# Sixteen maxima rounds of a gated mix kernel moved into a stage between the first up pairs

## The chip, the cores and the metric

The kernel runs on one core of one Trainium2 chip. The metric is the device time of one execution in microseconds. A core has five engines with a queue of instructions each: PE (TensorE, products; its weight loads are shown as PEld), DVE (VectorE), ACT (ScalarE), POOL (GpSimd) and SP (SyncE, which here issues nearly all DMAs). An engine works through its queue in program order, and an instruction waits on semaphores that other engines or DMAs raise.

## The reference

Input x has 2048 rows of 576. The output is `g * a + (1 - g) * b`:

```
g = sigmoid((x * gate_w).sum(-1))
a = softmax(q k^T * 18 ** -0.5) v @ wo          # 32 heads of 18; q, k, v = x @ wqkv
b = gelu(layernorm(x) @ w1 + b1) @ w2 + b2      # 576 -> 4608 -> 576, tanh form of gelu
```

All is float32.

## The kernel before, in words

A float32 product is made of three products of fp32r parts: each operand is split into a rounded part and the rest (`hh` and `hl`, or `t[:, 0]` and `t[:, 1]` of a weight), and rest times rest is left out.

**Front part** (to 250 us): four blocks `tb` = 0 to 3 of 512 rows. Each block has nine qk groups (lines 752 to 770: 14 products, the split by ACT and DVE, two writes to `qk_scr`) and eight v groups (lines 772 to 791: 14 products each, one tile of v written to `v_scr` after every second group). Between them the next block's x is transposed (line 687), the rows are normalized, and the normalized rows y are transposed, split and written to `y_scr` (lines 707 to 717, five `y_chunk`s a block).

**Maxima rounds.** The softmax needs each row's maximum ahead of the exponential. A round (`s1_round`, line 187) makes two score products of 512 columns (line 199) into the three banks of `ps_s1`, and DVE reduces each to maxima (line 201). There are 32 units (a pair of heads, half of the rows) of 32 rounds. After a unit's last round its maxima are transposed (line 216), read by ACT (line 218, tile `mr`) and written as rows into `qa` by DMA. The table `ROUNDS` puts the first 40 rounds into the front part: 10 in block 1, 14 in block 2, 16 in block 3, where they stand between the groups and share `ps_s1` with the transpositions. The other 984 stand in the loop.

**Loop** (from 250 us): 512 steps. A step makes two score products of 512 columns twice (`s2`, line 240, into the one two-bank tile `pss`) and their exponentials on ACT (line 242); every second step makes the products with v (`pv`, line 257). Rounds and pieces of the MLP stand between them.

**MLP** (`mlp`, line 326): a generator that yields after each slot of work with an estimate of its time; the loop takes pieces from it and paces them so that it ends at step 506 (`fill`, `behind`, `TOTAL`). For each of 36 chunks there are two *up pairs* (`h_pair`: two tiles of 512 columns of the hidden layer, 27 slots of two products at line 445) and four *out pairs* (`out_pair`, line 525). An up pair needs its split weight `W1[q]` and both parts of y: Y[0] (rounded) and Y[1] (rest), each a tile `big` loaded from `y_scr`. Y[1] gets the buffer that block 3's x holds until its last v group. After an up pair comes GELU on two tiles: bias (DVE and ACT, lines 465 and 466), Square on ACT, add and multiply on POOL (`plus`, recorded at line 156), Tanh on ACT, add and multiply on POOL, then the split into `hh` and `hl` on POOL. `open_pairs` lets one pair at a time be in GELU.

**Weights of the first 18 pairs** are split here: a raw chunk is loaded (`load_w1`, line 332; `load_w2`, line 338), ACT rounds it and POOL subtracts (`split`, lines 354 to 375, ACT at 361, POOL recorded at line 156). There is one raw tile R1 for W1, so the next chunk is loaded after POOL is done with the last. These steps, and all that is put off by `defer`, are recorded when `run_due` is called, which counts `slot`; in block 3 that is once for each round and once for each group from g = 9.

SP's DMAs use eight semaphores in turn, so a DMA's issue waits until the DMA eight places earlier has landed.

Of the kernel before, what the change touches and what calls it, by code (L numbers as in the profile page):

```python
# [8 lines left out]
F32 = mybir.dt.float32  # L9
# [35 lines left out]
PROJ = 7  # L45
EARLY = NSTEP - 40
ORDER = (0, 1, 3, 2)
ROUNDS = [lambda g: 0, lambda g: int(g >= 7), lambda g: int(g < 14), lambda g: int(g >= 4) + int(6 <= g < 9)]
SKIP = 0
N_AT = 5  # L50
W_AT = {0: 1, 1: 2, 3: 3, 5: 4, 7: 5}
# [5 lines left out]
def gated_mix_kernel(ctx: ExitStack, tc: tile.TileContext, x, wqkv, wo, w1, b1, w2, b2, gate_w, out):  # L57
# [39 lines left out]
    def psum(pool):  # L97
        return pool.tile([P, TB], F32, name="ps")
# [205 lines left out]
    def mlp():  # L304
# [112 lines left out]
        def cuts(n, pieces):  # L417

            return {(k * n + pieces - 1) // pieces for k in range(1, pieces)}

        def h_pair(q, last, inner=False):

            i, m, fc = chunk(q)
            tb = seq[i][0]
            while q == 0 and q not in W1:
                cut[0] = 3
                yield 0
            wt = ready(W1, q)
            del W1[q]
            ps = [psum(ps_w) for _ in range(2)]  # L430
            if q == 0:
                slots = [(w_, 0, c) for c in range(9) for w_ in (0, 1)] + [(0, 1, c) for c in range(9)]
            else:
                slots = [(w_, s_, c) for c in range(9) for w_, s_ in ((0, 0), (1, 0), (0, 1))]
            change = tb + 1 < NB and (q + 1) % (npair // NB) == 0
            loaded = 0
            late = spent[0] < behind[0]
            ends = cuts(27, (5, 5, 4)[piece[0]] if last else (3, 5, 4)[piece[0]])
            if (last or spent[0] > behind[0] + AHEAD) and piece[0] == 0 and not late:

                ends = {4, 9, 14, 18, 23}
            for k, (w_, s_, c) in enumerate(slots):
                for h in range(2):
                    r = slice(64 * h, 64 * h + 64)
                    nc.tensor.matmul(ps[h], wt[w_][r, c, :], Y[s_][r, c, :], start=(k == 0), stop=(k == 26))  # L445
                if change and (k + 1 in ends or k == 26):

                    load_y(tb + 1, 0, loaded, (k + 1) // 3)
                    load_y(tb + 1, 1, loaded, (k + 1) // 3)
                    loaded = (k + 1) // 3  # L450
                if k == 26:
                    break
                if k + 1 in ends:
                    cut[0] = 1
                yield 231
                while k == 25 and open_pairs[0]:
                    cut[0] = 3
                    yield 0
            open_pairs[0] = 1
            if inner:  # L460

                extra = wp1.tile([P, 2, 9, P], F32R, name="w4").rearrange("p a b c -> p (a b c)")
            zs = [zp.tile([P, TB], F32, name="z") for _ in range(2)]
            b = [b1t[:, fc + h:fc + h + 1] for h in range(2)]
            nc.vector.tensor_scalar(zs[1], ps[1], b[1], None, op0=ALU.add)
            nc.scalar.activation(zs[0], ps[0], AF.Identity, bias=b[0])
            for h in (1, 0):
                z = zs[h]
                w = zp.tile([P, TB], F32, name="zz", bufs=3)
                if inner:  # L470
                    hh, hl = [extra[:, (2 * h + k) * TB:(2 * h + k + 1) * TB] for k in range(2)]
                else:
                    hh = hp.tile([P, TB], F32R, name="hh")
                    hl = hp.tile([P, TB], F32R, name="hl")


                def plus(c, w, z):

                    pool_op(TB, nc.gpsimd.tensor_scalar, w, w, c, 1.0, op0=ALU.add, op1=ALU.mult)
                    pool_op(TB, nc.gpsimd.tensor_tensor, w, w, z, op=ALU.mult)  # L480

                def parts(w=w, z=z, hh=hh, hl=hl, h=h, j=2 * m + h):
                    plus(1.0, w, z)
                    rounded(hh, w)
                    pool_op(TB, nc.gpsimd.tensor_tensor, hl, w, hh.bitcast(F32), op=ALU.subtract)
                    queue_end(-1000.0, lambda: HT.update({(i, j): (hh, hl)}))
                    if h == 0:
                        open_pairs[0] = 0

                def first(w=w, z=z, parts=parts):  # L490

                    plus(GC0, w, z)
                    queue_end(200.0, lambda: second(w, parts))

                def second(w, parts):
                    nc.scalar.activation(w, w, AF.Tanh, scale=GC1)
                    defer(2, parts)
                defer(2, lambda w=w, z=z: nc.scalar.activation(w, z, AF.Square))  # L498
                defer(4 - h, first)
            cut[0] = 2  # L500
            yield 231
# [83 lines left out]
        for i in range(n + 1):  # L585
            q = 2 * i
            inside = i < n and seq[i][1] == NG - 1
            held = 1 if 0 < i < n and seq[i][1] == 0 else 2
            if i < n:
# [8 lines left out]
            if i < n and not inside:  # L598
                yield from pair(q + 1, held)

    opening = []
# [21 lines left out]
    def filler(upto):  # L623
# [8 lines left out]
                break  # L632
        run_due()


    mstack = ExitStack()
    with ExitStack() as a:
# [175 lines left out]
        for tb in range(NB):  # L813
            work = [(qk_group, (tb, mt)) for mt in (range(9) if tb < 2 else (4, 0, 1, 2, 3, 5, 6, 7, 8))] + [(v_group, (tb, t, n)) for t in range(4) for n in range(2)]
            for g, (fn, args) in enumerate(work):
# [22 lines left out]
                if tb == NB - 1:  # L838
                    if g == 1:
                        load_k(0, 3 * TB, S)  # L840
                    if g == 2:
                        load_q(1)
                        next(stream[0])
                    if g == 9:
                        qkstack.close()
                        wp1 = mstack.enter_context(tc.tile_pool(name="m_w1", bufs=3))
                        wp2 = mstack.enter_context(tc.tile_pool(name="m_w2", bufs=4))
                        next(stream[0])

# [5 lines left out]
                    if g == 7:  # L855
                        ps = psum(ps_s1)
                        nc.tensor.transpose(ps[:, :NFC], b1r, ident[:NFC, :NFC])
                        nc.vector.tensor_copy(b1t, ps[:, :NFC])
                if tb == 1 and g == 4:
                    load_q(0)  # L860
                    load_k(0, 0, TB)
# [1 line left out]
                    load_k(0, TB, 2 * TB)  # L863
                if tb == 2 and g == 3:
                    load_k(0, 2 * TB, 3 * TB)
                for _ in range(ROUNDS[tb](g)):
                    next_round()
                    run_due()
# [206 lines left out]
    for u in range(NU):  # L1075
        for kc in range(NT):
            step = u * NT + kc
            if kc == 1:
                if u + 2 < NU:
                    load_q(u + 2)  # L1080
                if u % 2 == 0 and u // 2 + 1 < NPAIR - 1:
                    load_k(u // 2 + 1)
                    load_v(u // 2 + 1)
                elif u == NU - 5:
                    load_k(NPAIR - 1)
                elif u == NU - 4:
                    load_v(NPAIR - 1)
            at[0] = step

            next_round()  # L1090
            s2(u, kc, 0)
            run_due(462.0)
            if kc % 2:
                fill(step, 1)
            elif step > 0:
                pv(step - 2)
                while ROWS:
                    ROWS.pop(0)()
                run_due(2080.0)
            if kc % 2:  # L1100
# [36 lines left out]
```

## Time and profile before

| | |
|---|---|
| median of 3 runs | 2357.26 us (2355.15 to 2359.28) |
| profiled execution | 2358.74 us |
| its span | 2356.8 us |
| granted clock of PE, mean | 0.996 |
| PE, DVE, ACT, POOL busy | 98%, 70%, 58%, 41% |

In the views, a row of a timeline has start, duration, engine, line, operation, output tile <- inputs, shapes and count; in brackets stands the engine's idle time before it and what ended that. A row of the table by stages has, for each engine, busy us and the number of instructions, then the granted clock of PE as a share of full speed, the busy share of the DMA engines and GB/s.

### The profile page before, as it was taken

What the parts mean: (1) busy time and instruction counts of PE and PEld (TensorE: products, weight loads), DVE (VectorE), ACT (ScalarE), POOL (GpSimd) and SP (SyncE); (2) the same over time, 40 slices, a digit from 0 to 9 for tenths busy, and PEclk for the clock granted to TensorE, in tenths of its full rate; (3) what the DMA queues carried; (4) which work ended last, traced back from release to release, by engine and by line L of the source; (5) the groups of instructions that cost most, each with busy time, mean ns of one, the idle gap of its engine ahead of it and who ended that gap; (6) DMA issues with size and microseconds to landing.
All of it is one profiled execution on the core that took longest, in us unless ns stands there. A gap on an engine that the chain in (4) does not pass through costs nothing.

```text
span 2356.8 us, 50607 instructions
## 1 busy us (share of the span) xinstructions
PE 2305.6 (98%) x20585; PEld 1613.7 (68%) x20585; DVE 1651.2 (70%) x2890; ACT 1366.8 (58%) x1604; POOL 971.2 (41%) x966
## 2 busy tenths in 40 slices
PE   8998899999999999999999999999999999999999
PEld 6876566666666666676666666666666666666658
DVE  5675577777777777777777777777777777777525
ACT  4222467666666666666665666666666666666661
POOL 4000466666554533333352444444445333333430
PEclk9999999999999999999999999999999999999999
DMA  7746945535455434232444433233354243322345
GB/s 232 248 149 193 275 138 177 175 132 149 135 155 156 157 95 117 95 114 95 127 137 130 160 114 117 94 117 115 117 160 150 94 117 110 102 95 99 131 139 198
DMA packets 164718, 330.40 MB, mean 140 GB/s; under 512 B 57822, under 2 KB 84482, under 8 KB 153650
## 3 DMA queue, kind: packets, MB, share of 16 engines
q1 hardware_dynamic: 161494, 321.71, 43.8%
q10 hardware_dynamic: 2992, 5.46, 0.6%
q8 instruction: 162, 2.65, 0.5%
q14 instruction: 70, 0.57, 0.1%
HBM read 234.31 MB, written 96.73 MB: 140 GB/s over the span
## 4 chain that ended last, share of the span: by engine, by line
PE 88%; DVE 4%; ACT 2%; DMA 2%; issue 2%; POOL 1%; SPq 1%; ACTq 0%; DVEq 0%; POOLq 0%
PE ps L525 20%; PE ps L257 19%; PE ps L445 17%; PE pss L240 13%; PE ps L199 11%; PE ps L763 4%; PE ps L781 2%; DVE m L201 1%; PE ps L1028 1%; ACT p L242 1%; POOL zz L156 1%; PE ps L687 1%; ACT w L361 1%; DMA wraw<-in_B_w_dram 0%; POOL w L156 0%
## 5 line engine op out<-in xcount | busy, mean ns | idle before, releaser
L201 DVE TENSOR_REDUCE m<-ps 128x1 f32<-128x512 f32 x2048 | 1298.3, 684 | 444.3 <-PE ps L199 442.4
L242 ACT ACTIVATE p<-pss 128x1024 f32<-128x1024 f32 x684 | 701.9, 1026 | 459.3 <-PE pss L240 446.8
L156 POOL TENSOR_SCALAR zz<-zz 128x512 f32<-128x512 f32 x288 | 179.7, 624 | 836.3 <-ACT zz L498 737.8
L445 PE MATMUL ps<-big,w 64*128 64x512 f32 x3888 | 520.2, 393 | 3.2 <-DMA big<-y_scr 3.1
L525 PE MATMUL ps<-w,hh 64*128 64x288 f32 x4352 | 495.4, 299 | 11.6
L240 PE MATMUL pss<-qa,ka 56*128 56x512 f32 x2048 | 479.5, 436 | 11.7 <-ACT p L242 7.8
L242 ACT ACTIVATE ring<-pss 128x1024 f32<-128x1024 f32 x340 | 348.9, 1026 | 231.6 <-PE pss L240 226.2
L199 PE MATMUL ps<-ka,qa 54*128 54x512 f32 x2048 | 457.3, 409 | 6.2 <-DVE m L201 2.6
L525 PEld LDWEIGHTS ps<-w,hh 64*128 64x128 f32 x4352 | 396.7, 185 | 67.5 <-issue 44.5
L445 PEld LDWEIGHTS ps<-big,w 64*128 64x128 f32 x3888 | 394.2, 185 | 67.6 <-DMA big<-y_scr 3.8
L156 POOL TENSOR_TENSOR zz<-zz,z 128x512 f32<-128x512 f32 x288 | 372.2, 1292 | 24.0
L240 PEld LDWEIGHTS pss<-qa,ka 56*128 56x128 f32 x2048 | 196.6, 184 | 265.8 <-ACT p L242 126.5
L525 PE MATMUL ps<-w,hl 64*128 64x288 f32 x2176 | 346.7, 292 | 0.0
L257 PE MATMUL ps<-p,vt 128*32 128x512 f32 x2736 | 346.2, 601 | 0.0
L199 PEld LDWEIGHTS ps<-ka,qa 54*128 54x128 f32 x2048 | 239.5, 185 | 36.1 <-DVE m L201 12.0
L525 PEld LDWEIGHTS ps<-w,hl 64*128 64x128 f32 x2176 | 231.4, 185 | 0.5
L156 POOL TENSOR_TENSOR w<-x,w 128x1152 fp32r<-128x1152 f32 (+1 forms) x36 | 73.1, 2045 | 324.8 <-ACT w L361 293.7
L156 POOL TENSOR_TENSOR hl<-zz,hh 128x512 fp32r<-128x512 f32 x136 | 176.9, 1300 | 11.3
L257 PE MATMUL ps<-ring,vt 128*32 128x512 f32 x1360 | 179.1, 598 | 0.0
L257 PEld LDWEIGHTS ps<-p,vt 128*32 128x32 f32 x2736 | 71.5, 109 | 149.0 <-issue 148.6
L534 DVE SCALAR_TENSOR_TENSOR x<-ps,x 128x288 f32<-128x288 f32 x256 | 105.2, 452 | 42.4 <-PE ps L525 28.7
L763 PE MATMUL ps<-big,wqk 128*128 128x512 f32 x504 | 125.2, 401 | 1.1 <-DVE wqk L681 0.9
(95 smaller groups left out, 1368.2 us busy)
## 6 DMA issues: line engine op xcount, KB each, us to landing
w<-w_scr SPq DMA_DIRECT2D x54, 1152.0 KB
w<-w_scr SPq DMA_DIRECT2D x108, 576.0 KB
w_scr<-w SPq DMA_DIRECT2D x18, 1152.0 KB
w_scr<-w SPq DMA_DIRECT2D x36, 576.0 KB
big<-y_scr SPq DMA_DIRECT2D x42, 384.0 KB
x<-in_B_w_dram SPq DMA_DIRECT2D x54, 288.0 KB
qa<-qk_scr SPq DMA_DIRECT2D x192, 72.0 KB
ka<-qk_scr SPq DMA_DIRECT2D x90, 144.0 KB
```

What stands on the lines that cost most here:

```text
L156: fn(*args, **kw)
L199: nc.tensor.matmul(ps, qa[r0:r0 + 54, t * P:(t + 1) * P], ka[r0:r0 + 54, kb * TB:(kb + 1) * TB], start=True, stop=True)
L201: nc.vector.tensor_reduce(M4[u][:, h, t, kb:kb + 1], ps, axis=AX.X, op=ALU.max)
L240: nc.tensor.matmul(ps[:, h, :], ka[r0:r0 + 56, kc * P:(kc + 1) * P], qa[r0:r0 + 56, qb * TB:(qb + 1) * TB], start=True, stop=True)
L242: nc.scalar.activation(RING[n % 3][:, qb], ps, AF.Exp, scale=SCALE)
L257: nc.tensor.matmul(OB[u][r:r + 32, :], v[:, k, 19 * h:19 * h + 32], RING[c % 3][:, qb, h, :], start=(k == 0), stop=(k == NT - 1))
L361: nc.scalar.activation(t[:, 0], src(), AF.Copy)
L445: nc.tensor.matmul(ps[h], wt[w_][r, c, :], Y[s_][r, c, :], start=(k == 0), stop=(k == 26))
L525: nc.tensor.matmul(ps[nn][:, :ND], h_[r, tok], w_[p_][r, cs[nn]], start=(k == 0), stop=(k == 6 * G - 1))
L534: nc.vector.scalar_tensor_tensor(dst, ps[nn][:, :ND], 0.5, b2b[:, cs[nn]] if g == 0 else dst, op0=ALU.mult, op1=ALU.add)
L763: nc.tensor.matmul(ps, w_[:, c, ms], big[:, s_, :], start=(k == 0), stop=(k == len(prods) - 1))
L781: nc.tensor.matmul(ps[:, :ND], big[:, s_, tok], w_[:, c, cs], start=(k == 0), stop=False)
```

## The change

- Block 3 has no rounds (`ROUNDS`). Its 16 rounds stand in a new stage between the front part and the loop: after each round the stage takes two stretches of about 600 ns (by the generator's estimates) from the MLP.
- The first two up pairs are made by `first_pairs`: the 18 slots with Y[0] of pair 0, then those of pair 1, then the nine slots with Y[1] of each. Pair 0 has the two banks of `ps_w`, pair 1 the two-bank tile `pss`. Pair 2 follows by `h_pair` in the same stage.
- GELU is a function of its own, `gelu`. For pairs recorded ahead of the loop (`early`), the two sums stand on ACT, as copies with a bias, instead of POOL.
- b1's transposition moves from block 3 to block 2, two W2 chunks are due three slots later, and step 0 of the loop takes one more piece.

```
-ROUNDS = [lambda g: 0, lambda g: int(g >= 7), lambda g: int(g < 14), lambda g: int(g >= 4) + int(6 <= g < 9)]
+ROUNDS = [lambda g: 0, lambda g: int(g >= 7), lambda g: int(g < 14), lambda g: 0]
...
                 load_w2(c)
+                LOADED[2, c] += 3
...
+        def banks(wide):
+
+            if wide:
+                ps = ps_s2.tile([P, 2, TB], F32, name="pss")
+                return [ps[:, h, :] for h in range(2)]
+            return [psum(ps_w) for _ in range(2)]
+
+        def first_pairs():
+
+            ps = {}
+            for q, slots in ((0, range(18)), (1, range(18)), (0, range(18, 27)), (1, range(18, 27))):
+                while q in (0, 1) and q not in W1:
+                    cut[0] = 3
+                    yield 0
+                if q not in ps:
+                    ps[q] = banks(q == 1)
+                wt = W1[q]
+                for k in slots:
+                    w_, s_, c = (k % 2, 0, k // 2) if k < 18 else (0, 1, k - 18)
+                    for h in range(2):
+                        r = slice(64 * h, 64 * h + 64)
+                        nc.tensor.matmul(ps[q][h], wt[w_][r, c, :], Y[s_][r, c, :], start=(k == 0), stop=(k == 26))
+                    if k < 26:
+                        yield 231
+                if k < 26:
+                    continue
+                while open_pairs[0]:
+                    cut[0] = 3
+                    yield 0
+                del W1[q]
+                yield from gelu(q, ps[q], False)
+                prep(q + 3)
...
+            early = not looped[0]
...
                 def plus(c, w, z):
 
-                    pool_op(TB, nc.gpsimd.tensor_scalar, w, w, c, 1.0, op0=ALU.add, op1=ALU.mult)
+                    if not early:
+                        pool_op(TB, nc.gpsimd.tensor_scalar, w, w, c, 1.0, op0=ALU.add, op1=ALU.mult)
                     pool_op(TB, nc.gpsimd.tensor_tensor, w, w, z, op=ALU.mult)
...
                     nc.scalar.activation(w, w, AF.Tanh, scale=GC1)
+                    if early:
+                        nc.scalar.activation(w, w, AF.Copy, bias=1.0)
...
+                    nc.scalar.activation(w, z, AF.Square)
+                    if early:
+                        nc.scalar.activation(w, w, AF.Copy, bias=GC0)
...
+    def stretch(ns):
+
+        upto = spent[0] + ns
+        while stream and spent[0] < upto:
+            spent[0] += next(stream[0])
+            end, cut[0] = cut[0], 0
+            if end == 3:
+                break
...
     while len(rounds) > NU * NR - NR - 2 * LEAD:
         next_round()
-        run_due()
+        run_due(233.0)
+        for part in range(2):
+            t = spent[0]
+            stretch(600.0)
+            run_due(max(spent[0] - t, 500.0))
```

How the instructions stand in a row shows in two places. The first is PE where the loop began: before, the last products of block 3 (line 784) are followed by block 3's last two rounds (line 199) and the loop's first scores (line 240), and pair 0 (`w_2108` is its weight) comes in pieces of 18 products between the loop's work.

```order
L784 MATMUL ps<-wv_126,big 128x288
L199 MATMUL ps<-ka_106,qa_104 128x512 x4
L240 MATMUL pss<-qa_103,ka_106 128x512 x4
L199 MATMUL ps<-ka_106,qa_104 128x512 x2
L445 MATMUL ps<-big,w_2108 128x512 x18
L199 MATMUL ps<-ka_106,qa_104 128x512 x2
L240 MATMUL pss<-qa_103,ka_106 128x512 x2
L445 MATMUL ps<-big,w_2108 128x512 x18
```

In the changed program (line 837 is the v group's last product, line 443 the product of `first_pairs`, `w_2189` pair 0's weight, `w_2276` pair 1's) the same place reads:

```order
L837 MATMUL ps<-wv_126,big 128x288
L199 MATMUL ps<-ka_106,qa_103 128x512 x2
L443 MATMUL ps<-big,w_2189 128x512 x12
L199 MATMUL ps<-ka_106,qa_103 128x512 x2
L443 MATMUL ps<-big,w_2189 128x512 x12
L199 MATMUL ps<-ka_106,qa_103 128x512 x2
L443 MATMUL ps<-big,w_2189 128x512 x12
L199 MATMUL ps<-ka_106,qa_103 128x512 x2
L443 MATMUL pss<-big,w_2276 128x512 x12
L199 MATMUL ps<-ka_106,qa_103 128x512 x2
```

Pair 1's first product now stands behind four rounds and 36 products; line 240 comes first after 16 rounds and 160 up products.

The second place is SP at the end of the front part. Before, in this order: pair 1's raw W1 (line 332), a raw W2 chunk (line 338), writes of v and y, W2, the rows of unit 0's maxima, and more writes; pair 2's raw W1, two v writes and the six loads of Y[1] (line 111, `big<-y_scr`) come next.

```order
L332 DMA x<-in_B_w_dram 64x9x128 x2
L338 DMA x<-in_B_w_dram 128x576
L791 DMA v_scr<-vt_109 128x832
L715 DMA y_scr<-hh 128x512
L715 DMA y_scr<-hl 128x512
L338 DMA x<-in_B_w_dram 128x576
L111 DMA qa_103<-mr 1x8x128 x4
L715 DMA y_scr<-hh 128x512
L715 DMA y_scr<-hl 128x512
L791 DMA v_scr<-vt_110 128x832
```

In the changed program (line 844 writes v, line 770 the last y chunk), from the last y chunk on:

```order
L770 DMA y_scr<-hh 64x512
L770 DMA y_scr<-hl 64x512
L338 DMA x<-in_B_w_dram 128x576 x2
L844 DMA v_scr<-vt_109 128x832
L844 DMA v_scr<-vt_110 128x832
L111 DMA big<-y_scr 64x3x512 x6
L332 DMA x<-in_B_w_dram 64x9x128 x2
L338 DMA wraw<-in_B_w_dram 128x576 x2
L185 DMA vt_109<-v_scr 128x16x52
L332 DMA x<-in_B_w_dram 64x9x128 x2
```

Pair 1's raw W1 has moved from ahead of the last y writes to behind the six loads of Y[1]; the second line-332 row is pair 2's, which waits until POOL has split pair 1's.

More of the change, by code (lines that the diff above doesn't have):

```diff
@@ L424, in h_pair @@
             tb = seq[i][0]
-            while q == 0 and q not in W1:
-                cut[0] = 3
-                yield 0
             wt = ready(W1, q)
             del W1[q]
[L430 to L434, printed above, removed]
+            ps = banks(False)
+            slots = [(w_, s_, c) for c in range(9) for w_, s_ in ((0, 0), (1, 0), (0, 1))]
             change = tb + 1 < NB and (q + 1) % (npair // NB) == 0
@@ L458, in h_pair, with gelu @@
                     yield 0
+            yield from gelu(q, ps, inner)
+        def gelu(q, ps, inner):
+            i, m, fc = chunk(q)
+            early = not looped[0]
             open_pairs[0] = 1
@@ L496, in second, with square @@
                     nc.scalar.activation(w, w, AF.Tanh, scale=GC1)
+                    if early:
+                        nc.scalar.activation(w, w, AF.Copy, bias=1.0)
                     defer(2, parts)
-                defer(2, lambda w=w, z=z: nc.scalar.activation(w, z, AF.Square))
+                def square(w=w, z=z):
+                    nc.scalar.activation(w, z, AF.Square)
+                    if early:
+                        nc.scalar.activation(w, w, AF.Copy, bias=GC0)
+                defer(2, square)
                 defer(4 - h, first)
@@ L588, in mlp @@
             held = 1 if 0 < i < n and seq[i][1] == 0 else 2
-            if i < n:
+            if i == 0:
+                yield from first_pairs()
+            elif i < n:
                 yield from pair(q, held, last=i > 0)
@@ L597, in mlp @@
                 prep_w2(i)
-            if i < n and not inside:
+            if 0 < i < n and not inside:
                 yield from pair(q + 1, held)
@@ L854, in gated_mix_kernel @@
                         nc.vector.tensor_scalar(gate1, gate, -1.0, 1.0, op0=ALU.mult, op1=ALU.add)
[L855 to L858, printed above, removed]
                 if tb == 1 and g == 4:
@@ L865, in gated_mix_kernel @@
                     load_k(0, 2 * TB, 3 * TB)
+                if tb == 2 and g == 13:
+                    ps = psum(ps_s1)
+                    nc.tensor.transpose(ps[:, :NFC], b1r, ident[:NFC, :NFC])
+                    nc.vector.tensor_copy(b1t, ps[:, :NFC])
                 for _ in range(ROUNDS[tb](g)):
@@ L1099, in gated_mix_kernel @@
                 run_due(2080.0)
+            else:
+                fill(step, 2)
             if kc % 2:
```

## The prediction, made before the changed kernel was run

> **What bounds the kernel now.** I read the page first: engines and the costliest groups. In each row the number before the comma is the group's busy time in us.
>
> ```profile
> PE 2305.6 (98%) x20585; PEld 1613.7 (68%) x20585; DVE 1651.2 (70%) x2890; ACT 1366.8 (58%) x1604; POOL 971.2 (41%) x966
> L445 PE MATMUL ps<-big,w 64*128 64x512 f32 x3888 | 520.2, 393 | 3.2 <-DMA big<-y_scr 3.1
> L525 PE MATMUL ps<-w,hh 64*128 64x288 f32 x4352 | 495.4, 299 | 11.6
> L240 PE MATMUL pss<-qa,ka 56*128 56x512 f32 x2048 | 479.5, 436 | 11.7 <-ACT p L242 7.8
> L199 PE MATMUL ps<-ka,qa 54*128 54x512 f32 x2048 | 457.3, 409 | 6.2 <-DVE m L201 2.6
> L257 PE MATMUL ps<-p,vt 128*32 128x512 f32 x2736 | 346.2, 601 | 0.0
> ```
>
> PE is busy 98% of the span, and the change leaves every one of its products in place. It can win only what PE now loses: idle time and time at a lower clock. So the second view is the table by stages (after the engines: granted clock, DMA share, GB/s).
>
> ```profile
> 195.00:214.00 19.00, 16.43 (x63) 10.68 (x61) 15.39 (x37) 2.48 (x5) 0.00 (x0) 1.00 1.00 221
> 214.00:223.00 9.00, 7.19 (x27) 4.81 (x28) 6.06 (x12) 1.09 (x2) 0.00 (x0) 0.94 0.99 349
> 223.00:235.00 12.00, 9.70 (x54) 8.82 (x53) 5.20 (x12) 5.47 (x9) 5.36 (x3) 0.78 0.27 86
> 250.00:268.00 18.00, 11.91 (x73) 8.29 (x73) 7.45 (x12) 6.57 (x8) 4.96 (x3) 0.86 1.02 241
> 268.00:296.00 28.00, 27.61 (x204) 16.70 (x204) 14.74 (x23) 17.04 (x21) 20.95 (x23) 0.91 0.95 298
> 1000.00:1400.00 400.00, 397.47 (x3777) 272.73 (x3771) 296.61 (x515) 245.08 (x279) 162.99 (x172) 1.00 0.39 120
> ```
>
> In the loop PE idles 2.5 us in 400. The losses lie in block 3 with its 16 rounds (195 to 235: 6.7 us idle, the clock at 0.78 in its last 12) and at the loop's start (250 to 268: 6 us idle, clock 0.86). Just these two places are rebuilt. Note the DMA column: full from 195 to 223 and from 250 on.
>
> **Block 3 without rounds.** Five qk groups stand without a round; v groups stand with a y transposition in block 0 and without one in block 2.
>
> ```profile
> 180.80 16.48 PE L763 MATMUL ps<-big,wqk 128*128 128x512 f32 x70
> 54.45 1.58 PE ps L781 x12
> 56.73 1.59 PE ps L781 x12
> 177.25 1.59 PE ps L781 x12
> 179.12 1.58 PE ps L781 x12
> 250.14 0.59 PE L240 MATMUL pss<-qa,ka 56*128 56x512 f32 x2
> ```
>
> Nine groups at 16.48/5 = 3.3 are 29.7; one transposition 0.5; four v groups at 2.28 and four at 1.87 are 16.6. From 181.0, with 0.5 for the b1 transposition that now stands ahead, the block ends near **228.3** instead of 250.1. Of these 21.8 us, the rounds' own products (32 by 457.3/2048 = 0.223, with their transposition 7.4 in all) only move.
>
> **Break-even.** From 250.1 to the end of the third pair's products, PE does 162 up products at 520.2/3888 = 0.134, 34 of line 240 at 0.234, 32 of line 199 at 0.223 and 48 of line 257 at 0.127: 42.9 us of work.
>
> ```profile
> 291.11 1.56 PE L445 MATMUL ps<-big,w 64*128 64x512 f32 x12
> 292.51 0.40 PE L199 MATMUL ps<-ka,qa 54*128 54x512 f32 x2
> 294.61 1.32 PE L445 MATMUL ps<-big,w 64*128 64x512 f32 x10
> ```
>
> It takes until 295.9, so 2.9 us are lost by these averages. The changed program, up to its first 12 out products (at 495.4/4352 = 0.114), has the same 162, 40 of line 199, 8 of line 240: 34.2 us with the transposition. If it gets there at time t, it stands t - 34.2 + 7.4 - 250.1 - 2.9 = **t - 279.8** us behind before. The stage and the loop's first steps may take until 279.8 before anything is lost.
>
> **What the stage waits for.** PE meets pair 1 after four rounds and 36 products of pair 0, and pair 1's weights are asked for only after the six Y loads. SP's DMAs land in the order of issue: the two halves of Y's first load, issued at 197.6, came at 208.85 and 214.30, when the waits on them ended.
>
> ```profile
> 197.62 1.28 SPq L111 DMA_DIRECT2D big<-y_scr  x2
> 203.80 0.77 SPq L770 DMA_DIRECT2D qk_scr<-hl  x1
> 208.85 0.32 SPq L769 DMA_DIRECT2D qk_scr<-hh  x1
> 214.30 0.32 SPq L770 DMA_DIRECT2D qk_scr<-hl  x1
> big<-y_scr SPq DMA_DIRECT2D x2, 1152.0 KB
> big<-y_scr SPq DMA_DIRECT2D x42, 384.0 KB
> x<-in_B_w_dram SPq DMA_DIRECT2D x54, 288.0 KB
> qk_scr<-hh SPq DMA_DIRECT2D x36, 256.0 KB
> v_scr<-vt SPq DMA_DIRECT2D x16, 416.0 KB
> ```
>
> At 214 some 2.9 MB of qk writes wait (the window 195 to 214 moved 4.2 MB, of which 3.5 are loads). Block 3 still writes y (2.4 MB) and four v tiles (1.7). Before, these were spread to 249; now they are produced by 229. 7.0 MB at the 349 GB/s of the row 214 to 223 take 20 us: to 234. Two W2 chunks (0.59 MB at 221 GB/s) go to 237, Y's second half (2.36 MB; its twin took 5.05 + 5.45 us) to 247.4, pair 1's W1 (0.59 MB) to **250.1**. Then come ACT's rounding and POOL's subtraction:
>
> ```profile
> 249.47 1.17 ACT L361 ACTIVATE w<-x 128x1152 fp32r<-128x1152 f32 x1 [2.75 <-DMA x<-in_B_w_dram]
> 250.71 2.63 POOL L156 TENSOR_TENSOR w<-x,w 128x1152 fp32r<-128x1152 f32 x1 [7.49 <-ACT w L361]
> ```
>
> Pair 1's rounded part is there at 251.3, its rest at 253.9.
>
> **The stage, step by step.** In a stretch without waits an up product starts every 0.117 us (12 in 1.40, rows 291.11 and 292.51) and a round adds 0.24. Pair 0's own W1 split on ACT stands behind the last v eviction, which needs the v tile's write landed (231): rounded part 232.7, rest 235.3. So PE idles to 235.3, works to 240.0, idles to 253.9. Behind the waiting product stand rounds 5 to 16 (so DVE too), pair 0's second part and the exponentials; nothing on PE can pass it. Pair 1's first slots and rounds 5 to 7 end at 261.1, with 2.5 us for a cold clock, as it cost before after the idle stretch at 262:
>
> ```profile
> 268.00:271.00 3.00, 3.00 (x18) 0.59 (x16) 0.00 (x0) 2.06 (x3) 1.56 (x3) 0.50 0.51 153
> 271.00:274.00 3.00, 3.00 (x20) 1.94 (x18) 1.13 (x2) 1.54 (x2) 2.67 (x3) 0.66 1.00 164
> ```
>
> (Three us at 0.50 and three at 0.66 lose 2.5.) The Trainium skill, "TensorE: Matmul & The Clock Gate", part 1, says that an idle window of about 3.4 us halves the clock and a busy one of 3.4 us frees it: an estimate of 1.7 us lost, which would make the sum 0.8 less; the rows above show more.
>
> The Y slots of both pairs end at 266.1, rounds 10 to 12 at 269.5 (they share three banks with the transposition that ACT reads after four GELU steps). Pair 2's weights are loaded once POOL has freed the raw tile at 253.9; by the same rates they land near 258 and are split by 262, in time. Its 52 products and five rounds end near 277.2. Then the exponentials start, each behind GELU steps and behind the next W1's load on ACT:
>
> ```profile
> L242 ACT ACTIVATE p<-pss 128x1024 f32<-128x1024 f32 x684 | 701.9, 1026 | 459.3 <-PE pss L240 446.8
> L156 POOL TENSOR_TENSOR zz<-zz,z 128x512 f32<-128x512 f32 x288 | 372.2, 1292 | 24.0
> L156 POOL TENSOR_SCALAR zz<-zz 128x512 f32<-128x512 f32 x288 | 179.7, 624 | 836.3 <-ACT zz L498 737.8
> L498 ACT ACTIVATE zz<-z 128x512 f32<-128x512 f32 x144 | 82.5, 626 | 0.0
> ```
>
> Four of them (1.03 each), four GELU steps (0.63) and a bias step among them, with 1.2 us of waiting for W1, put the twelfth out product at **t = 286.4**. The eight sums that move cost POOL 8 x 0.624 less and ACT 8 x 0.63 more, if a copy with a bias is priced as its neighbour Square (bounds: nothing, and the exponential's 1.03); they lie beside PE's waits, and without that cover at most 8 x 0.4 = 3.2 us come on top. The b1 transposition, the fill in step 0 and the raised due time of two W2 chunks I price at nothing: PE has other products queued there, or waits anyway. Unit 2's q and k loads move behind the writes of the split weights, but keep their distance to the rounds that use them, which start later as well.
>
> Later the loop has three pairs fewer to do. That is work taken over, counted above; PE's 2.5 us in 400 leave little to win or lose, and I take 0 (bounds -3 and +3).
>
> Sum: 286.4 - 279.8 = **+6.6 us** on the profiled execution's 2358.74, so 2365.3; that execution lay 1.5 above the median of 2357.26. I predict 2365.
>
> **Rivals.** *The stage does its work* (faster). If the queue is empty when Y's load is issued at 229 and everything flows at 349 GB/s, Y and W1 (2.95 MB) land by 237.5 and pair 1 is split by 241.3: t = 273.8, -6.0 us, 2353. It decides from pair 1 being split before 247.3. For it: two of the four idle places of before vanish. Against it: the full DMA column, and Y's halves at 216 to 234 GB/s.
>
> *Reads faster than Y's first load showed*, behind the same writes: 2.95 MB from 237 at 349 GB/s land 4.7 us earlier, +1.9 us, 2361. The waits before also allow it: there W2's chunk, issued right behind Y, was complete 16.0 us after Y's first issue:
>
> ```profile
> 249.67 3.88 SPq L111 DMA_DIRECT2D big<-y_scr  x6
> 265.67 0.68 ACT w L361
> ```
>
> From an issue at 229 that gives 245 and about +1.5. The Trainium skill, "DMA: Bandwidth & Descriptors", Bandwidth, measured 341 GB/s at 1 MB; by that figure, as an estimate, the sum would be +2.1. The trace does not agree so far for 1.18 MB loads.
>
> *The delay spreads* (slower still): a second cold stretch, then GELU of two pairs queued on POOL (about 9 us each by the rows above) ahead of the out products: some 6 us more, +13, 2372.
>
> **Chances.** Forecast (+4.7 to +10) 0.46; reads faster, within 0.2% (4.7 us, about what can be told from no change) 0.30; the stage works 0.12; the delay spreads 0.12. So faster 0.12, same 0.30, slower 0.58. The range from 2352 to 2371 leaves out the far ends of the last two.
>
> **What would show it.** Right: block 3's last v product near 228; PE idle for 10 us or more ahead of the first product into pss by line 443, released by ACT's split of W1; a clock under 0.8 behind it; the first line-240 product at 275 to 280; DMA share near 1 from 195 to 250. Wrong: that product before 247, or a block 3 that ends past 232 because evictions wait for landed writes.

## The result, and the profile after

The changed kernel takes 2372.97 us (median of 4 runs, 2371.89 to 2373.63) and the kernel before beside it 2358.27 (2355.15 to 2360.88): a ratio of 1.0061 [1.0048, 1.0074], 14.7 us slower. Beside later experiments it was run again: 2373.99 us, 1.0064 [1.0051, 1.0077]. The direction was forecast; the 2365 us were 8 short, and the upper bound of 2371 was 2 short.

The profiled execution has a span of 2370.9 us, 14.1 above that of before. The page's engine row:

```profile
PE 2307.9 (97%) x20585; PEld 1619.7 (68%) x20585; DVE 1653.4 (70%) x2890; ACT 1369.7 (58%) x1612; POOL 964.4 (41%) x958
```

PE is busy 2.3 us longer with the same number of products, more of them at a lower clock; the other 11.8 us are idle time. The table by stages, cut at the places that the prediction names:

```profile
195.00:214.00 19.00, 19.00 (x97) 15.99 (x96) 11.60 (x30) 3.09 (x6) 0.00 (x0) 1.00 0.99 212
214.00:229.00 15.00, 14.08 (x106) 13.36 (x104) 5.16 (x11) 6.44 (x12) 2.83 (x2) 1.00 1.05 397
229.00:240.00 11.00, 5.63 (x32) 4.15 (x34) 2.99 (x6) 1.46 (x2) 2.61 (x1) 0.69 1.01 294
240.00:255.00 15.00, 4.51 (x26) 3.01 (x24) 2.54 (x4) 2.31 (x3) 4.83 (x3) 0.67 0.84 172
255.00:275.00 20.00, 18.38 (x118) 13.47 (x118) 14.59 (x26) 9.88 (x16) 11.40 (x10) 0.82 0.84 292
1000.00:1400.00 400.00, 397.52 (x3756) 271.70 (x3754) 297.62 (x514) 246.95 (x280) 162.66 (x172) 1.00 0.41 124
```

Block 3 without rounds runs at full speed: PE is busy 33.1 of 34 us to 229, at a clock of 1.00. Then PE idles 15.9 us in 26, and the clock falls to 0.67. The loop is what it was. PE's timeline of the stage, with the waits in brackets:

```profile
227.74 0.51 PE L199 MATMUL ps<-ka,qa 54*128 54x512 f32 x2
232.47 0.80 PE L443 MATMUL ps<-big,w 64*128 64x512 f32 x2 [4.22 <-ACT w L362]
235.16 2.50 PE L443 MATMUL ps<-big,w 64*128 64x512 f32 x10 [1.90 <-POOL w L156]
...
250.15 0.79 PE L443 MATMUL pss<-big,w 64*128 64x512 f32 x2 [8.59 <-ACT w L362]
252.84 2.50 PE L443 MATMUL pss<-big,w 64*128 64x512 f32 x10 [1.90 <-POOL w L156]
...
277.89 0.62 PE L240 MATMUL pss<-qa,ka 56*128 56x512 f32 x2
...
286.82 0.44 PE L567 MATMUL ps<-w,hl 64*128 64x288 f32 x2
```

And what held pair 1, on ACT: its raw weights landed at 248.9.

```profile
248.93 1.16 ACT L362 ACTIVATE w<-x 128x1152 fp32r<-128x1152 f32 x1 [16.51 <-DMA x<-in_B_w_dram]
```

This is the stage as it was forecast, row by row (below). But it explains half of the 14.1 us. To see where the rest arises, take the **lag**: the start of a step's first exponential, less its start in the kernel before. At step 480 both kernels have done the same products of every kind (counted in the traces), so the lag there needs no correction. Before, then after:

```profile
2176.08 1.02 ACT L242 ACTIVATE p<-pss 128x1024 f32<-128x1024 f32 x1 [0.72 <-PE pss L240]
```

```profile
2183.72 1.02 ACT L242 ACTIVATE p<-pss 128x1024 f32<-128x1024 f32 x1 [0.72 <-PE pss L240]
```

The lag is **7.6 us** at step 480, the spans differ by **14.1**: 6.5 us are lost in the last 32 steps and behind the loop, 1900 us after the stage. The program's order says what differs there: the MLP's last product stands at step 504, not 506, and 70 of the output projection's 448 products by line 1081 stand inside the loop, not 49. The pacing sets that place: it spreads what is left of the MLP over the loop's steps, counted from the work done when the loop begins, and in the runs below its constant alone moves the end between 504 and 506. Which part of the change tipped it (the pairs made early, or the piece more in step 0) no run separates.

### The profile page after: what moved, and what is told of

Read it like the earlier page. It is cut to its first block, busy times and chain, and to the rows that moved or that the text cites. A ratio compares the mean times of both kernels' runs of the same rounds, so it can differ in the third digit from the quotient of the medians.

```text
span 2370.9 us, 50656 instructions
## 1 busy us (share of the span) xinstructions
PE 2307.9 (97%) x20585; PEld 1619.7 (68%) x20585; DVE 1653.4 (70%) x2890; ACT 1369.7 (58%) x1612; POOL 964.4 (41%) x958
## 4 chain that ended last, share of the span: by engine, by line
PE 89%; DVE 4%; DMA 3%; ACT 2%; issue 1%; POOL 0%; SPq 0%; DVEq 0%; ACTq 0%; POOLq 0%
PE ps L567 20%; PE ps L257 19%; PE ps L473 18%; PE pss L240 13%; PE ps L199 11%; PE ps L816 4%; PE ps L834 2%; PE ps L1081 1%; DVE m L201 1%; ACT p L242 1%; DMA x<-in_B_w_dram 1%; DMA qk_scr<-hl 1%; PE ps L740 1%; DVE p L800 0%; DMA dn_scr<-dn 0%
## 5 line engine op out<-in xcount | busy, mean ns | idle before, releaser
L156 POOL TENSOR_SCALAR zz<-zz 128x512 f32<-128x512 f32 x280 | 173.7, 620 | 845.2 <-ACT zz L537 749.9
L473 PE MATMUL ps<-big,w 64*128 64x512 f32 x3780 | 507.5, 393 | 0.0
L473 PEld LDWEIGHTS ps<-big,w 64*128 64x128 f32 x3780 | 386.1, 186 | 59.1
L567 PEld LDWEIGHTS ps<-w,hl 64*128 64x128 f32 x2176 | 235.3, 185 | 0.3
L156 POOL TENSOR_TENSOR w<-x,w 128x576 fp32r<-128x576 f32 (+1 forms) x36 | 73.1, 2042 | 335.7 <-ACT w L362 329.6
```

Source lines behind the costliest of these rows:

```text
L156: fn(*args, **kw)
L567: nc.tensor.matmul(ps[nn][:, :ND], h_[r, tok], w_[p_][r, cs[nn]], start=(k == 0), stop=(k == 6 * G - 1))
```

## The experiments

All twelve runs in one table, below the changed kernel's first. Lag at the end is the span less 2356.8; the column behind it is what was added after step 480. In each of the twelve the products done by step 480 are the same as before. Each lag is read from one profiled execution: two of the changed kernel give 7.6 and 6.9, and y1_split3 and three_mended, whose order is the same up to step 400, differ by 1.4 us at step 384. The intervals of the ratios are 2 to 3 us wide to each side, so the times alone don't tell y1_behind_w1, half_rounds_back and one_pair from the changed kernel; there the timelines decide.

| run | median us | ratio to before | MLP ends at step | lag at 480 | lag at the end | added behind 480 |
|---|---|---|---|---|---|---|
| changed kernel | 2372.97 | 1.0061 [1.0048, 1.0074] | 504 | 7.6 | 14.1 | 6.5 |
| changed_again | 2373.99 | 1.0064 [1.0051, 1.0077] | 504 | 6.9 | 13.2 | 6.3 |
| after_mlp_506 | 2374.62 | 1.0068 [1.0055, 1.0080] | 506 | 15.9 | 17.4 | 1.5 |
| before_mlp_504 | 2364.62 | 1.0024 [1.0015, 1.0033] | 504 | -0.4 | 4.9 | 5.3 |
| tail_506 | 2366.31 | 1.0032 [1.0021, 1.0042] | 506 | 7.6 | 7.7 | 0.1 |
| y1_behind_w1 | 2370.76 | 1.0052 [1.0039, 1.0066] | 504 | 5.5 | 11.3 | 5.8 |
| y1_split3 | 2367.23 | 1.0032 [1.0021, 1.0043] | 504 | 2.8 | 7.8 | 5.0 |
| half_rounds_back | 2369.52 | 1.0046 [1.0034, 1.0059] | 504 | 5.2 | 10.7 | 5.5 |
| one_pair | 2371.51 | 1.0051 [1.0039, 1.0064] | 504 | 4.3 | 14.1 | 9.8 |
| gelu_sums_pool | 2381.48 | 1.0099 [1.0086, 1.0113] | 504 | 17.1 | 23.2 | 6.1 |
| three_mended | 2359.50 | 1.0002 [0.9993, 1.0010] | 506 | 0.7 | 0.3 | -0.4 |
| half_mended | 2358.16 | 0.9997 [0.9988, 1.0006] | 506 | -1.2 | -1.6 | -0.4 |
| half_mended_one_pair | 2356.17 | 0.9990 [0.9981, 0.9999] | 506 | -3.0 | -3.5 | -0.5 |

The theory: the stage costs some 7 us through pair 1's late weights, and the MLP's end at 504 costs some 6 more. The rival: the stage costs all, and the end only shows it.

### The end of the MLP, both ways

after_mlp_506:

```
-FIN = NSTEP - 6
+FIN = NSTEP - 5
```

> The changed kernel with one constant of the pacing moved (FIN = NSTEP - 5), so that the MLP's last product stands at step 506 of 512 again, as in the kernel before, and not at 504; 21 products of the output projection then move from the loop's last steps to behind it. Theory A (about half of the loss was made at the end of the loop: projection products that stand ahead of the last exponentials delay them, and what follows the last exponential is a chain of transfers that doesn't get shorter): 2366 to 2368 us, 5 to 7 below the changed kernel's 2373, and the last exponential about 4 us earlier. Theory B (the whole loss comes from the new stage and its delay is only carried to the end): 2372 to 2374, no difference.

before_mlp_504, on the kernel before:

```
-FIN = NSTEP - 6
+FIN = NSTEP - 8
```

> The kernel before with the pacing constant moved the other way (FIN = NSTEP - 8): the MLP's last product at step 504, as in the changed kernel, and no new stage. Theory A (the end of the MLP at step 504 costs by itself): 2362 to 2365 us, 4 to 7 above the kernel before. Theory B (the end costs nothing, the stage costs all): 2357 to 2359.

The kernel before at 504 costs 5.5 us (2364.62 against 2359.09 beside it), all of it behind step 480: A holds. The changed kernel at 506 did not get faster: 2374.62 us lies outside A's range and 0.6 above B's. Its table row says why: behind step 480 it adds 1.5 us and not 6.5, but ahead of it it lost 8 more. 7.2 of them arise between steps 320 and 384, at both of which it has done the same products as the changed kernel, and one long wait stands there, at step 368. PE, then SP, in after_mlp_506:

```profile
1748.75 1.17 PE L240 MATMUL pss<-qa,ka 56*128 56x512 f32 x2 [4.26 <-DMA qa<-mr]
```

```profile
1729.93 4.22 SPq L111 DMA_DIRECT2D big<-y_scr  x3
1735.41 6.83 SPq L111 DMA_DIRECT2D qa<-mr  x4
```

The same place on SP in the changed kernel, where PE's score product did not wait:

```profile
1724.98 10.22 SPq L111 DMA_DIRECT2D big<-y_scr  x12
1735.30 2.80 SPq L111 DMA_DIRECT2D qa<-mr  x4
```

At the MLP's third change of block, Y is loaded in pieces as its buffers come free. With the other pacing the pair that frees them stands later, the loads run up to the unit's change at step 368, and the four row loads of the new unit's maxima take 6.83 us to issue and not 2.80. The next score product waits 4.26 us and PE then runs at half its clock:

```profile
1740.60:1747.40 6.80, 3.82 (x46) 3.17 (x43) 4.90 (x9) 2.05 (x2) 2.61 (x3) 1.00 1.01 203
1747.40:1754.20 6.80, 5.45 (x22) 1.84 (x24) 0.64 (x1) 1.02 (x1) 0.00 (x0) 0.50 0.02 6
```

So the run mixed two effects. The next one keeps every instruction ahead of step 400 where the changed kernel has it.

tail_506:

```
-            behind[0] = base + (TOTAL - base) * step / FIN
+            behind[0] = base + (TOTAL - base) * step / (FIN if step < 400 else FIN + 1)
```

> The changed kernel with the pacing constant raised by one only from step 400 on, so that every instruction ahead of step 400 stands where the changed kernel has it, and the MLP ends at step 506 in place of 504. The run with the constant raised from the start mixed two things: its end was 6 us shorter, and it got a new 4.3 us wait at step 368, where the block's loads of Y had moved in front of the next unit's four row loads. Theory A (the end of the MLP at 504 costs about 6 us by itself): 2366 to 2368 us, the steps up to 480 within 0.5 us of the changed kernel, and no wait on qa<-mr over 1 us at step 368. Theory B (what the end gives up comes back elsewhere): 2372 to 2374.

2366.31 us, 6.7 below the changed kernel; the lag is 7.6 at step 480 and 7.7 at the end. A holds, B is out: the end costs some 6.5 us by itself. How it costs them, the last steps show. On ACT, the changed kernel:

```profile
2304.42 1.02 ACT L242 ACTIVATE p<-pss 128x1024 f32<-128x1024 f32 x1 [0.65 <-PE pss L240]
2305.34 1.66 ACT L1014 ACTIVATE big<-x 128x512 fp32r<-128x512 f32 x3
2307.84 0.63 ACT L1014 ACTIVATE big<-x 128x512 fp32r<-128x512 f32 x1 [0.84 <-DVE x L1011]
2308.38 1.01 ACT L242 ACTIVATE p<-pss 128x1024 f32<-128x1024 f32 x1
```

and tail_506:

```profile
2301.72 1.02 ACT L242 ACTIVATE p<-pss 128x1024 f32<-128x1024 f32 x1 [0.66 <-PE pss L240]
2303.40 1.03 ACT L242 ACTIVATE p<-pss 128x1024 f32<-128x1024 f32 x1 [0.66 <-PE pss L240]
```

The projection's preparation (line 1014) begins two steps earlier and stands on ACT ahead of the last exponential, which starts 4.0 us after the one before it and not 1.7. Then SP's queue, the changed kernel and the kernel before:

```profile
2316.69 0.38 SPq L982 DMA_DIRECT2D x<-ot_scr  x1
2317.12 0.68 SPq L982 DMA_DIRECT2D ka<-ot_scr  x1
2317.90 0.66 SPq L281 DMA_DIRECT2D dn_scr<-dn  x1
2326.85 0.64 SPq L286 DMA_DIRECT2D ot_scr<-dn_scr  x1
```

```profile
2304.49 0.35 SPq L281 DMA_DIRECT2D dn_scr<-dn  x1
...
2307.66 0.65 SPq L286 DMA_DIRECT2D ot_scr<-dn_scr  x1
2308.42 0.43 SPq L929 DMA_DIRECT2D x<-ot_scr  x1
2308.90 0.70 SPq L929 DMA_DIRECT2D ka<-ot_scr  x1
```

The last unit's softmax sums (`dn`, 8 KB) go to DRAM and come back spread (line 286). Before, they go ahead of the two loads of 1 MB each by line 929; now they go behind them, and the step from issue to the next takes 8.95 us and not 3.17. In the changed kernel's chain of work that ended last (start, duration), that landing is the wait:

```profile
2317.90 8.93 DMA dn_scr<-dn
```

tail_506 has the order of before again: the sums at 2312.13, their return at 2315.30, the loads from 2316.05. PE runs out of projection products that it may do, in the changed kernel (first row) for 4.77 us, in tail_506 (second row) for 1.39, and in the changed kernel its clock halves on top (the stages):

```profile
2339.82 2.77 PE L1081 MATMUL ps<-big 128*128 128x288 f32 x10 [4.77 <-DVE res L1090]
```

```profile
2339.67 1.59 PE L1081 MATMUL ps<-big 128*128 128x288 f32 x10 [1.39 <-DVE res L1090]
```

```profile
2337.60:2341.00 3.40, 1.18 (x5) 1.18 (x6) 3.10 (x7) 1.69 (x3) 0.00 (x0) 0.50 0.91 240
2341.00:2344.40 3.40, 3.40 (x16) 3.40 (x16) 3.40 (x7) 1.87 (x4) 0.00 (x0) 0.50 0.84 272
```

The longer wait is 3.4 us, and the 4.6 us of products at a clock of 0.50 lose about 2.3 more (an estimate from these rows): 5.7 of the 6.5. No run moved the 8 KB alone or the preparation on ACT alone, so what each of them is worth is not shown.

before_mlp_504 shows the same order: there its loads stand at 2308.93 and 2309.37, the sums at 2310.12, and their return is issued at 2319.21.

### The order of two loads, and what stood behind it

y1_behind_w1 takes the three `load_y(0, 1, c, c + 3)` out of `mlp`'s opening and puts them behind pair 1's raw weights:

```
                 nc.sync.dma_start(R1[64 * h:64 * h + 64], src.rearrange("(c p) n -> p c n", p=64))
+            if q == 1:
+                for c in range(0, 9, 3):
+                    load_y(0, 1, c, c + 3)
```

> The changed kernel with one order on SyncE's queue changed: the six loads of Y's second part (big<-y_scr) are issued behind the two loads of pair 1's raw W1, not ahead of them. Theory A (PE's idle 8.6 us before the first product into pss is pair 1's raw W1 waiting its turn behind 2.4 MB of Y): raw W1 of pair 1 lands near 240.5 in place of 248.9, the first product into pss starts near 242 in place of 250.2, the first line-240 product at 268 to 272 in place of 277.9, and the time is 2364 to 2367 us, 6 to 9 below the changed kernel. Theory B (the wait only changes its name: PE then waits for Y's second part, or for the GELU of pair 0): the first line-240 product stays at 275 to 279 and the time at 2371 to 2374.

The stage did what A says. PE (line 446 is the changed kernel's 443):

```profile
241.93 0.50 PE L446 MATMUL pss<-big,w 64*128 64x512 f32 x2
...
271.89 0.62 PE L240 MATMUL pss<-qa,ka 56*128 56x512 f32 x2
278.33 0.80 PE L240 MATMUL pss<-qa,ka 56*128 56x512 f32 x2 [5.82 <-ACT p L242]
```

The wait of 8.6 us is gone, and line 240 begins 6.0 us earlier. But the second line-240 product starts 2.5 us earlier than the changed kernel's 280.87, no more, and the time is 2370.76 us, 2.2 lower, where A named 2364 to 2367. PE now waits for an exponential, which is late on ACT:

```profile
276.20 1.16 ACT L365 ACTIVATE w<-x 128x1152 fp32r<-128x1152 f32 x1 [1.32 <-DMA x<-in_B_w_dram]
277.27 1.00 ACT L242 ACTIVATE p<-pss 128x1024 f32<-128x1024 f32 x1
```

Pair 3's split stands on ACT ahead of the first exponential and waits for its own raw weights. They land at 276.2; in the changed kernel they land at 278.7, the same 2.5 us later. So A has the wait and its cause right, but another wait takes its place, as B has it; it is one that B did not name.

y1_split3 has, besides, that split put off behind the first eight exponentials:

```
-            LOADED[1, q] = slot[0] + (LAND if looped[0] else 6)
+            LOADED[1, q] = slot[0] + (LAND if looped[0] else 18 if q == 3 else 6)
```

> The changed kernel with Y's second part behind pair 1's raw W1 (as in the run before) and the split of pair 3's W1 on ScalarE put behind the first eight exponentials and not ahead of them. Theory A (what was won in the stage, first line-240 product at 271.9 and not 277.9, was given back by the first exponential, which stood on ScalarE behind a split that waited until 276.2 for its raw weights): the second line-240 product at 273 to 275 in place of 278.3, and 2366 to 2368 us, 3 to 5 below the run with Y's order alone (2370.8). Theory B (the out products of the first chunk, which need pair 1's hidden tiles, end last anyway): 2370 to 2372.

2367.23 us, 3.5 lower and in A's range; the lag at 480 is 2.8. The second line-240 product starts at 276.48, 1.9 earlier than without, but later than the 273 to 275 of A: the exponential ahead of it now stands on ACT behind a Tanh that waits for GpSimd until 274.22. A holds for the time: of the stage's 7.6 us these two orders are 4.8.

one_pair makes the first two pairs in full, one after the other:

```
-            for q, slots in ((0, range(18)), (1, range(18)), (0, range(18, 27)), (1, range(18, 27))):
+            for q, slots in ((0, range(27)), (1, range(27))):
```

> The changed kernel with the first two pairs made one after the other in full, and not their first 18 slots each and then their last 9. Theory A (pair 0's last nine slots need only Y's second part, which lands ahead of pair 1's raw W1, so they fill 2 to 3 us of PE's 8.6 us wait): the first product into pss stays near 250, the first line-240 product comes 2 to 3 us earlier, near 275, and the time is 2369 to 2372. Theory B (Y's second part lands no earlier than pair 1's weights, or the last GELU ends last): 2372 to 2375.

```profile
246.08 1.64 PE L443 MATMUL ps<-big,w 64*128 64x512 f32 x5 [1.11 <-DMA big<-y_scr]
250.42 0.79 PE L443 MATMUL pss<-big,w 64*128 64x512 f32 x2 [2.70 <-ACT w L362]
...
275.23 0.63 PE L240 MATMUL pss<-qa,ka 56*128 56x512 f32 x2
```

Pair 0's last nine slots fit into the wait, and the lag at 480 is 4.3 us, 3.3 less: A holds for the stage. The time, 2371.51, is only 1.5 lower; in the profiled execution (2372.73, 1.2 above the median) the last steps added 9.8 us. There the clock fell to half in the first projection products:

```profile
2276.50:2279.90 3.40, 2.17 (x17) 1.39 (x13) 0.00 (x0) 2.05 (x2) 0.00 (x0) 0.99 0.90 273
2279.90:2283.30 3.40, 3.40 (x15) 2.25 (x19) 0.52 (x1) 1.02 (x1) 0.00 (x0) 0.50 1.02 380
2283.30:2286.70 3.40, 3.40 (x16) 0.52 (x16) 0.00 (x0) 1.02 (x1) 0.00 (x0) 0.50 1.00 296
```

The changed kernel idles the same 1.18 us there, between the MLP's end and the projection's start (PE is busy 2.22 us of the 3.40 from 2278.80), at a clock of 1.00.

### Half the rounds, and the GELU sums

half_rounds_back:

```
-ROUNDS = [lambda g: 0, lambda g: int(g >= 7), lambda g: int(g < 14), lambda g: 0]
+ROUNDS = [lambda g: 0, lambda g: int(g >= 7), lambda g: int(g < 14), lambda g: int(g >= 10)]
...
-            stretch(600.0)
+            stretch(1400.0)
```

> The changed kernel with eight of the sixteen rounds put back into block 3 (its groups from 10 on), and two and a third times as many up products between the rounds that are left, so that both first pairs still end ahead of the loop. The last v product then comes about 4 us later, near 231 to 232. Theory A (the rounds in block 3 covered transfers that end when they end: pair 1's raw W1 lands near 250 in both): the first line-240 product comes 3 to 4 us earlier, near 274, and the time is 2369 to 2371. Theory B (the stage is bound by PE's own work, which only moves): 2372 to 2374, the first line-240 product near 278.

2369.52 us is in A's range, and the lag at 480 falls from 7.6 to 5.2, but A's account of it is wrong. Block 3's last v product comes at 236.9, not 231 to 232, and pair 1's weights do not land near 250: the first product into pss starts at 242.98 without a wait, and line 240 at 266.5. Rounds inside block 3 let pair 0's split be recorded there (ACT does it at 227.78, not 231.27), and so pair 1's raw weights are asked for ahead of Y[1], as in y1_behind_w1, on SP:

```profile
231.72 1.34 SPq L332 DMA_DIRECT2D x<-in_B_w_dram  x2
233.16 4.89 SPq L844 DMA_DIRECT2D v_scr<-vt  x2
238.14 3.88 SPq L111 DMA_DIRECT2D big<-y_scr  x6
```

Then PE waits 3.02 us for an exponential that stands behind GELU steps on ACT, and 5.89 us, ahead of the third line-240 pair at 278.80, for one that stands behind the same split of pair 3.

gelu_sums_pool has `early = False`, so that the first pairs' sums are on GpSimd again:

> The changed kernel with the two GELU sums of the early pairs back on GpSimd, the rest of the change kept. The theory is that GpSimd, which does 1.3 us per product of two tiles, is the longer of the two engines in this stretch (it is busy from 266.3 to 278 without a gap over 0.2 us), so four more sums of 0.62 us each for a pair delay the hidden tiles of pair 1 by 2 to 3 us; the twelfth out product needs them, and the time rises by 1 to 3 us, to 2374 to 2376. The rival, that PE has other work beside it and the rounding of pair 2's W1 ends last: no difference, 2372 to 2374.

2381.48 us, 8.5 above the changed kernel, far over the 1 to 3 expected. The lag splits it. At step 320, where both kernels have done the same products, it is 16.7 us against the changed kernel's 13.5, a difference of 3.2 that is there, as 3.4, at step 32 already: the sums cost 3.2 in the stage, at the edge of what was expected. At step 384, again with equal products, it is 19.6 against 9.6: 6.7 more come from one wait of 3.8 us on `qa<-mr` at step 368, the one of after_mlp_506, with the cold clock behind it. The part of the change that moved the sums is worth its 3 us; the other part came by pacing.

### All of it together

three_mended is y1_split3 with tail_506's pacing; half_mended is half_rounds_back with pair 3's split put off and that pacing; half_mended_one_pair has one_pair's order in addition; changed_again is the changed kernel itself.

> The changed kernel with three orders mended at once and nothing else: Y's second part behind pair 1's raw W1, pair 3's split behind the first exponentials, and the MLP's end at step 506. If the losses of the stage (4.6 us won by the first two) and of the end (6.5 us) are independent and nothing else is lost: 2373 - 5 - 6.5, 2360 to 2363 us, 1 to 3 above the kernel before. If the parts share their gain (the end had slack that the stage's delay filled): 2364 to 2367.

> The kernel with eight of the moved rounds back in block 3, with pair 3's split behind the first exponentials and the MLP's end at 506. In the run with the eight rounds alone the first pair's weights were split inside block 3, the first product into pss came at 243.0 without a wait, the first line-240 product at 266.5, and then PE stood 3.0 and 5.9 us behind exponentials that waited on ScalarE behind the split of pair 3. Theory A (that split is all that is left of the loss): 2356 to 2360 us, level with the kernel before. Theory B (the GELU of pair 1 on GpSimd ends last and holds the first out products): 2361 to 2364.

> The kernel of the run half_mended with the first two pairs made one after the other in full. Theory A (pair 0's GELU then starts some 5 us earlier and the hidden tiles of the first chunk are ready sooner): 1 to 2 us below half_mended. Theory B (pair 0 then waits for Y's second part, which lands near 252, and that wait is worth as much): 0 to 3 us above it.

> The changed kernel as it is, beside the three others on one chip, so that differences of a few us have a base of their own: 2371 to 2374 us, ratio 1.0045 to 1.0075 to the kernel before.

three_mended comes to 2359.50 us, level with the kernel before (1.0002), 14.5 below changed_again on the same chip: the two losses add. It is a little lower than the 2360 to 2363 expected, and alone the two mends gave 5.7 and 6.7. The 2.1 us over stand in the lag at step 480, 0.7 where y1_split3 has 2.8. 1.4 of them are there at step 16 already, with the same order; the granted clock from 229 to 296 is 0.82 and not 0.77. So most of it is a difference between two executions, not one of the orders. half_mended is level too, as A said. half_mended_one_pair is 2.0 us lower still, as its A said, though the two intervals overlap: with 0.9990 [0.9981, 0.9999] it is the only version of the twelve whose interval lies below the kernel before, by 0.1%, half of the 0.2% that the prediction takes for about what can be told from no change. The change as such has little in it even with its orders mended.

## Why the prediction was right and wrong

By its own steps:

- **Block 3 without rounds** ends near 228.3: its last v product ends at 227.8. Right.
- **Pair 0's weights**, rounded 232.7, rest 235.3: PE's products on them start at 232.47 and 235.16. Right.
- **Pair 1's weights** land at 250.1, rounded 251.3, rest 253.9: 248.9, 250.1, 252.8. Right to 1.2 us, partly by luck, for two errors nearly cancel: the backlog drained faster than at the 349 GB/s assumed (397 from 214 to 229), and Y's six loads were issued at 231.9, behind SP's wait for v writes, not at 229. The rival "reads faster" named 245.4 for this landing, 4.7 us ahead of the forecast; 1.2 of them came.
- **Pair 2 and the rounds** end at 277.2: the first line-240 product starts at 277.89. **The twelfth out product** at t = 286.4: it ends at 287.26. With the break-even of 279.8 that is +7.5, and the lag at step 480 is 7.6. (The trace of before has 32 products of line 240 from 250.1 to 295.9, not 34; with 32 the break-even is 280.3, the forecast +6.1 and this reading +7.0.) Right: the stage costs about what was said, by the wait that was said. y1_behind_w1 shows that the order of two loads makes the wait; of the loss that order alone gives back 2.1 us, with pair 3's split 4.8, because other waits stand right behind it.
- **Its signs** came but for one: PE idles 8.59 us ahead of the first product into pss (and 1.90 more two products later), where 10 or more were named.
- **The GELU sums** were priced at nothing where they now stand on ACT. Back on GpSimd they cost 3.2 us of the stage, so the move is worth about 3 us, which the prediction gave no separate credit.
- **"Later the loop has three pairs fewer to do. That is work taken over, counted above; PE's 2.5 us in 400 leave little to win or lose, and I take 0 (bounds -3 and +3)."** This step failed. For the loop up to step 480 it holds within 1 us (6.7 at step 8, from a lag of 19.4 less 192 out products done ahead at 0.066 us, since 18 of them start within 1.19 us near 1742; 7.6 at step 480). Behind it stood 6.5 us, over the bound of 3. The work that was taken over was counted, but not where the pacing lets it end. The order of the program had it before any run: last MLP product at 504 and not 506, 70 projection products inside the loop and not 49, and, as before_mlp_504 confirms, the 8 KB of sums behind 2 MB of loads on SP. With these 6.5 the sum is 6.6 + 6.5 = 13.1, of the 14.0 us between the two profiled executions.
- **The rival "the delay spreads"** gave 2372 by a second cold stretch and GELU on POOL. The time is near by luck. Cold stretches did follow (a clock of 0.84 from 275 to 296; before, 0.91 from 268 to 296), but the stage's own loss was 7.6 and not 13.

The stage's rows were read closely because the change was written there. The pacing reads the work done so far and turned an edit at 250 us into another order at 2280.

## What to carry to other kernels

Where an edit changes how much work is done by some point, and a pacer or planner reads that amount, compare the instruction order of every queue up to the last row, above all the end, not only around the edit. When a wait is taken away, ask what stands in order behind it on each queue: here a mended DMA order met a weight split ahead of the exponentials, and a mended pacing met a unit's change. A lag measured at points where two kernels have done the same work tells where time is lost; the total does not.

## What the runs showed of the hardware

- In one_pair PE idled 1.23 of 3.40 us, and its granted clock stood at 0.50 for the next 6.8 us (the three rows above). The same 1.18 us gap in the changed kernel cost no clock. The Trainium skill, "TensorE: Matmul & The Clock Gate", part 1, has free-running windows of about 3.4 us and only a full and a half clock. The three stretches of 0.50 behind step 300 whose rows stand above (after_mlp_506, one_pair, the changed kernel's end) are each 6.8 us long, two such windows, which agrees with that. The window ahead of a fall need not be idle throughout: in one_pair, if it is the stretch from 2276.50 to 2279.90, PE was busy for 64% of it. PE was then busy all through both windows at 0.50.
- The 8 KB of `dn`, issued right behind two loads of 1 MB each, kept the transfer that depends on it 8.95 us from its issue in the changed kernel and 9.09 in before_mlp_504; issued ahead of them, in the kernel before and in tail_506, it was 3.17 us.
